# A spectral filter and an MLP side by side: where one row load is issued, and which engine does six additions

## The chip, the cores and the metric

The kernel runs on one core of a Trainium2 chip. The core has five engines with a queue of instructions each: TensorE (PE, matrix products into PSUM, with its weight loads listed apart as PEld), VectorE (DVE), ScalarE (ACT), GpSimd (POOL) and SyncE (SP), which here issues all the DMAs. Each queue is executed in its written order; semaphores hold an instruction until what it reads is there. The metric is the time of one execution on the device in microseconds (us), as the median of several runs.

## The reference

The input x has 2048 rows of 448 numbers. Two branches read its layer norm and are added to it:

```python
x = A_x
xn = _layernorm(x, axis=-1)
return x + _A_ref(xn, A_w_r, A_w_i) + _B_ref(xn, B_w1, B_w2, B_w3, B_w4)
```

Branch A takes a real two-dimensional Fourier transform of xn, multiplies it by a filter and transforms it back. Branch B is an MLP over tokens and channels:

```python
h = _gelu(_layernorm(x, axis=-1) @ w1)
# the four quarters of h's columns are shifted by +1, -1, +2, -2 rows
x1 = x + concatenate([g0, g1, g2, g3], axis=-1) @ w2
return x1 + _gelu(_layernorm(x1, axis=-1) @ w3) @ w4
```

with w1, w2 of 448 x 448, w3 of 448 x 1792 and w4 of 1792 x 448.

## The kernel before

**Blocks and groups.** The 2048 rows are taken as 16 blocks of 128 (row 16a + b belongs to block b), kept in float32 in the tiles `xt`. Most products are made from float16 pairs, a high part (ACT) and the rest (DVE), in two or three passes.

**The opening.** SP issues the loads of x, w1, w2 and w3 in the first 12 us. Blocks are normed in four groups of four (`norm1`), turned, and multiplied by w1 (`w1_unit`, matmuls at L465). The gelu of each block goes as a float16 pair into a small tile `hs` (or a part of `x2mem`), and a transposing DMA (L492) brings it into `h`, from where the products with w2 (L510) take it with its shifts. While transposes are awaited, PE goes on with w1 of the next group.

**The second norm.** `ln2` norms the finished rows of some blocks and writes them as a pair into a staging tile `y`; a transposing DMA (L553) puts them into `x2mem`. Its record `after["b8"]` holds the last instructions of the call for blocks 8 to 11: one on ACT, one on DVE and the DMA transpose of block 11 on SP.

**The channel MLP.** Eight groups G = 0 to 7 of two blocks each take seven steps fp. `front` makes the products with w3 (L435), the gelu (L773) and its float16 pair `hf` (L776 on ACT, L777 on DVE). `back` makes the products with w4 into `acc` (L811). For groups 5 to 7 (`STR`), a scheme with fewer products is used: `forms` combines parts of `hf` into `hgm` (L786 to L788), products go into `cr` and `acc` (L826), and at the last such step `cr` is copied to `cross` (L843), four adds of 128 x 224 combine it (L846) and two adds of 128 x 448 bring it into the result (L850). What the title of the change calls group seven is the seventh of the eight, G = 6.

**The spectral branch.** Steps of it are put between those of the MLP. Each of eight folds takes two blocks: `do_fold` loads their rows of x again (L574), norms them on ACT (L578), and adds and subtracts mirrored columns on POOL (L583 to L586); `step1_in` makes the pair `xh` (L594, L595), and `step1` multiplies it (L604). The folds use four buffers in turn. Three, `xf`, lie in memory that w2 and `h` hold before; the fourth is laid over `hgm`, which is not used until group 5. Then come the products of each chunk of the spectrum, the filter, and the way back (`inv_a`, `inv_b`), at whose end a block's sum is written over its rows (L750), put together with a fresh load of x (L560) and stored.

**What sets the order.** A planner writes each engine's queue: it takes the program's instructions with their dependencies and priorities and simulates them with costs of its own. `prio(FILL)` marks the MLP as work that fills gaps; `prio(EVAC)` puts what empties PSUM first. `behind(key)` adds an order without a semaphore: an instruction in the block is queued after the recorded instruction of the same engine. `PACE` and `FOLD` tie the folds' products and norms so to steps of the MLP. An instruction with no such tie and no dependency can be queued as early as the planner finds its engine free. So it is with the rows of the fourth fold: nothing uses their buffer earlier, and the load stands in SP's queue right after the opening loads, at 11.72 us. Loads of folds one to three follow when their memory comes free, at 99.42 us, between the transposes of blocks 4 to 7 and those of blocks 8 to 11.

Of the kernel before, what the change touches and what calls it, by code (L numbers as in the profile page):

```python
# [16 lines left out]
ALU = mybir.AluOpType  # L17
AX = mybir.AxisListType

S, D, DF, F = 2048, 448, 225, 1792  # L20
# [102 lines left out]
def body(tc, nc, x, wf, w1, w2, w3, w4, c_g, c_n, c_small, out):  # L123
    V, A, P, T, SY = nc.vector, nc.scalar, nc.gpsimd, nc.tensor, nc.sync
    PSUM = bass.MemoryType.PSUM

    @contextlib.contextmanager
    def prio(base):
        kept = tc.cur_priority
        tc.cur_priority = max(base, at.get(base, 0))  # L130
        yield
        at[base] = tc.cur_priority
        tc.cur_priority = kept
# [19 lines left out]
    def bank(tag, name):  # L153
        return ps.tile([128, 512], F32, tag=tag, bufs=2, name=name)
# [10 lines left out]
    def xb(b):  # L165
        g, i = WHERE[b]
        return xt[g][:, i]

    xv = x.rearrange("(a b) d -> a b d", b=NB)
# [54 lines left out]
    cross = x2mem.bitcast(F32)[:, 4 * F:4 * F + 2 * D].rearrange("p (i n) -> p i n", i=2)  # L224
# [171 lines left out]
    after = {}  # L396

    @contextlib.contextmanager
    def behind(*key):
        key = key if len(key) > 1 else key[0]  # L400
        with contextlib.ExitStack() as st:
            for i in after[key]:
                st.enter_context(tc.issue_after(i))
            yield
# [166 lines left out]
    def do_fold(b0):  # L571
        f = xf_buf[b0 // 2 % 4]
        X = f.rearrange("p b s d -> p (b s d)")[:, 0:2 * D + 2].rearrange("p (b d) -> p b d", b=2)
        after["X", b0] = (SY.dma_start(X[:, :, 0:D], xv[:, b0:b0 + 2]).ins,)  # L574
        with behind("f", *FOLD[b0 // 2]):
            for i in range(2):
                x_ = X[:, i, 0:D]
                A.activation(out=x_, in_=x_, func=AF.Identity, scale=xn_scale[b0 + i], bias=xn_bias[b0 + i])  # L578
            A.activation(out=X[:, :, D:D + 1], in_=X[:, :, 0:1], func=AF.Copy)  # L579
        ad = X[:, :, 0:D].rearrange("p b (h d) -> p h b d", h=2)[:, :, :, 0:113]  # L580
        bc = X[:, :, 1:D + 1].rearrange("p b (h d) -> p h b d", h=2)[:, ::-1, :, 223:110:-1]
        u = xr.rearrange("p (a b s d) -> p a b s d", a=2, b=2, s=2)
        P.tensor_tensor(out=u[:, 0], in0=ad, in1=bc, op=ALU.add)  # L583
        P.tensor_tensor(out=u[:, 1], in0=ad, in1=bc, op=ALU.subtract)
        for k, op in ((0, ALU.add), (2, ALU.subtract)):
            i = P.tensor_tensor(out=f[:, :, k:k + 2].rearrange("p b s d -> p s b d"), in0=u[:, :, 0], in1=u[:, :, 1], op=op)  # L586
        after["fold", b0] = (i.ins,)
        for i in range(2):
            folds[b0 + i] = f[:, i].rearrange("p s d -> p (s d)")
# [165 lines left out]
    def crossed(G, fp):  # L755
        return G in STR and (G, fp) not in ((7, 5), (7, 6))
# [3 lines left out]
    def keep(m):  # L760
        after["s", len(slots)] = (m.ins,)
        slots.append(m)
# [28 lines left out]
    def back(G, fp):  # L791
        h = hs.pop((G, fp))
        n = D // 2
        end = 4 if G == 7 else 6
        if fp == 0:
            acc[G] = [bank("acc", f"acc{G}{i}") for i in range(2)]
            if G in STR:
                xs[G] = [bank("tr", f"cr{G}{i}") for i in range(2)]
        if (G, fp) == (7, 5):
            xs[G] = [bank("tr", f"end{i}") for i in range(2)]  # L800
        C = [[(slice(0, D), acc[G][i][:, 0:D], 0, 6)] for i in range(2)]
        if G == 7:
            C[1] = [(slice(0, D), acc[G][1][:, 0:D], 0, 4)]
            if fp > 4:
                C[1] = [(slice(n * k, n * k + n), xs[G][k][:, 0:n], 5, 6) for k in range(2)]
        for i in range(2):
            for r, to, s, e in C[i]:
                with behind("m", G, fp) if (G, fp) == (7, 6) and ("m", G, fp) in after else contextlib.nullcontext():
                    for f in range(2):
                        for hi, wi in ((0, 0),) if crossed(G, fp) else ((0, 0), (0, 1), (1, 0)):  # L810
                            m = T.matmul(to, h[:, hi, 2 * f + i], w4p[0][:, wi, 2 * fp + f, r],  # L811
                                         start=fp == s and f == 0 and hi + wi == 0, stop=fp == e and f == 1 and hi == 1)
                after["m", G, fp] = (m.ins,)
            if not i and not crossed(G, fp):
                yield keep(m)
        if crossed(G, fp):
            g = hg.pop((G, fp))
            X = [xs[G][k // 2][:, n * (k % 2):n * (k % 2) + n] for k in range(4)]
            H = [[acc[G][i][:, n * k:n * k + n] for k in range(2)] for i in range(2)]
            prods = [(0, 1, X[0], 9), (1, 3, H[1][0], 9), (3, 2, H[0][0], C[0][0][3]), (6, 4, X[2], 9),  # L820
                     (4, 5, X[3], end), (5, 6, X[1], end), (2, 7, H[1][1], C[1][0][3])]
            for hi, wi, part in ((0, 1, 0), (1, 0, 0), (0, 1, 1), (1, 0, 1)):
                if hi + part == 1 and wi == part:
                    yield keep(m)
                for k, slot, to, e in prods[3 * part:3 + 4 * part]:
                    m = T.matmul(to, h[:, hi, slot] if slot < 4 else g[:, hi, slot - 4], w4f[fp][k][wi], start=k in (0, 6) and fp == 0 and hi == 0,  # L826
                                 stop=hi == 1 and fp == e)
            after["m", G, fp] = (m.ins,)
        k34 = p34[:, 1:2] if G >= 6 else p34[:, 0:1]
        to = {i: rest[2 * G + i] if G >= 6 else xb(2 * G + i) for i in range(2)} if fp >= 4 else {}  # L830

        def evacuate(i):
            for r, src, _, e in C[i]:
                if fp == e:
                    V.scalar_tensor_tensor(out=to[i][:, r], in0=src, scalar=k34, in1=to[i][:, r], op0=ALU.mult, op1=ALU.add)
                    if G == 7 and fp == 6:
                        SY.dma_start(ov[:, 2 * G + i, r], to[i][:, r])

        with prio(EVAC):
            if G in STR and fp == end:  # L840
                e0, e1 = cross[:, 0], cross[:, 1]
                for i in range(2):
                    A.activation(out=cross[:, i], in_=xs[G][i][:, 0:D], func=AF.Copy, scale=k34)  # L843
                for o, x, y in ((e0[:, n:], e0[:, 0:n], e0[:, n:]), (e1[:, 0:n], e1[:, 0:n], e0[:, n:]),
                                (e0[:, n:], e0[:, n:], e1[:, n:]), (e1[:, n:], e1[:, 0:n], e1[:, n:])):
                    (V if G == 7 else P).tensor_tensor(out=o, in0=x, in1=y, op=ALU.add)  # L846
            for i in range(2):
                evacuate(i)
                if G in STR and fp == end:
                    (V if G == 7 else P).tensor_tensor(out=to[i], in0=to[i], in1=cross[:, 1 - i], op=ALU.add)  # L850
                if G == 6 and fp == 6:
                    SY.dma_start(ov[:, 2 * G + i], to[i])
        yield keep(m)

    def steps(Gs, last=False, hook=None, ahead=1, tags=("mm",)):
        todo = [(G, fp) for G in Gs for fp in range(7)]
        done = formed = 0
        for n, (G, fp) in enumerate(todo):
            while done < min(n + 1 + ahead, len(todo)):
                yield from front(*todo[done], tags[done % len(tags)])  # L860
                if hook:
                    with prio(EVAC):
                        hook(*todo[done])
                done += 1
            while formed < min(n + 2, len(todo)):
                forms(*todo[formed])
                formed += 1
            if fp == 3 and last:
                for b in (2 * G, 2 * G + 1):
                    rest[b] = unscaled(b, x2mem.bitcast(F32)[:, D * (b - 12):D * (b - 11)])  # L870
            yield from back(G, fp)
# [139 lines left out]
    for k in (1, 3):  # L1011
        with behind(0, 3):
            A.activation(out=w2p[:, 0, k], in_=w2s[:112, k], func=AF.Copy)
        with behind("np", 2):
            i = P.tensor_tensor(out=w2p[:, 1, k], in0=w2s[:112, k], in1=w2p[:, 0, k], op=ALU.subtract)
# [95 lines left out]
    for b in range(0, NB, 2):  # L1111
        do_fold(b)
        step1_in(b)
        step1_in(b + 1)
        with behind("m", *PACE[b // 2]):
            step1(b)
            step1(b + 1)
# [80 lines left out]
```

## Time and profile before

| | |
|---|---|
| median of three runs | 410.64 us (409.51 to 411.13) |
| the profiled execution | 409.72 us |
| its span, first to last instruction | 407.6 us |
| PE, DVE, ACT, POOL busy | 401.3, 304.2, 268.6, 179.8 us |
| granted TensorE clock, of full speed | 0.999 |
| moved by DMA | 49.46 MB |

The profile is one execution. The span is shorter than the time by what lies around the instructions. Busy time is the union of an engine's instructions; the matmuls of a stretch overlap in the records, since they are pipelined. A row of the timeline gives start and length in us, engine, line, operation, output and input tile, shape, the number of instructions merged, and in brackets the idle time before it with what ended it. A row of a group gives count, busy us and mean ns. DMA rows on SP show the issue; the landing times are given apart, from issue to the last byte.

### The profile page before, as it was taken

How to read it: one execution, taken by the hardware profiler on the slowest of the kernel's cores; microseconds unless marked ns; L12 is line 12 of the kernel's file. 1: busy time of each engine (PE TensorE's matmuls, PEld its weight loads, DVE VectorE, ACT ScalarE, POOL GpSimd, SP SyncE). 2: the span in 40 equal slices, each digit the busy share in tenths (PEclk: the TensorE clock that was granted, in tenths of full speed). 3: DMA queues.
4: the chain of work that ended last, by engine and by line, in shares of the span. 5: the costliest groups of instructions: out<-in, count | busy, mean ns of one | idle time of the engine just before them, and what ended most of it. 6: DMA issues, size and time to landing. Idle time of an engine off the chain costs nothing.

```text
span 407.6 us, 8828 instructions
## 1 busy us (share of the span) xinstructions
PE 401.3 (98%) x3379; PEld 296.0 (73%) x3379; DVE 304.2 (75%) x658; ACT 268.6 (66%) x465; POOL 179.8 (44%) x276
## 2 busy tenths in 40 slices
PE   8998999999999999999999999999999999999996
PEld 4553555666767777776888887877788888888885
DVE  5988999899653757894577777763488879889645
ACT  4698993884737865763488888785956566544332
POOL 3889723011197747499243344441231254217100
PEclk9999999999999999999999999999999999999999
DMA  8999999915910375317055666642000022323201
GB/s 282 351 274 198 177 180 261 260 23 109 207 48 0 92 233 175 103 36 170 19 135 146 151 145 151 153 112 60 2 2 2 24 68 75 108 70 112 92 2 45
DMA packets 57209, 49.46 MB, mean 121 GB/s; under 512 B 41312, under 2 KB 52192, under 8 KB 57168
## 3 DMA queue, kind: packets, MB, share of 16 engines
q1 hardware_dynamic: 57168, 48.91, 46.4%
q8 instruction: 26, 0.43, 0.5%
q14 instruction: 15, 0.12, 0.1%
HBM read 35.06 MB, written 3.67 MB: 95 GB/s over the span
## 4 chain that ended last, share of the span: by engine, by line
PE 96%; DMA 2%; ACT 1%; DVE 0%; issue 0%; ACTq 0%
PE pw L435 33%; PE acc L811 24%; PE pw L510 9%; PE pw L465 6%; PE cr L826 4%; PE acc L826 3%; PE pu L707 3%; PE ps L604 3%; PE pp L661 2%; PE pe L727 2%; PE px L678 2%; PE py L749 2%; PE wps L889 2%; DMA h<-hs 2%; PE pta L414 1%; PE end L811 1%
## 5 line engine op out<-in xcount | busy, mean ns | idle before, releaser
L435 PE MATMUL pw<-x2mem,w3p 128*128 128x256 f16 x1232 | 149.7, 272 | 0.0
L435 PEld LDWEIGHTS <-w3p 128*128 128x128 f16 x1232 | 118.7, 98 | 19.4
L811 PE MATMUL acc<-w4p,hf 128*128 128x448 f16 x508 | 107.4, 352 | 0.0
L811 PEld LDWEIGHTS <-hf 128*128 128x128 f16 x532 | 51.5, 98 | 35.5
L777 DVE SCALAR_TENSOR_TENSOR hf<-pw,h,hf 128x512 f16<-128x512 f32 x56 | 41.8, 747 | 36.5 <-ACT hf L776 36.3
L773 ACT ACTIVATE pw<-pw,pe 128x512 f32<-128x512 f32 x56 | 36.7, 656 | 44.8 <-PE pw L435 44.6
L510 PE MATMUL pw<-w2p,h 112*128 112x448 f16 x192 | 39.2, 353 | 1.3 <-DMA h<-hs 1.2
L734 POOL TENSOR_TENSOR e<-e 128x226 f32<-128x226 f32 x16 | 11.1, 696 | 63.7 <-ACT e L731 56.2
L776 ACT ACTIVATE hf<-pw,h 128x512 f16<-128x512 f32 x56 | 38.3, 683 | 1.3
L465 PE MATMUL pw<-w1p,w4x 128*128 128x448 f16 x176 | 34.8, 352 | 0.5 <-DVE h L967 0.5
L510 PEld LDWEIGHTS <-h 112*128 112x128 f16 x192 | 18.4, 98 | 18.0 <-DMA h<-hs 2.2
L688 POOL TENSOR_TENSOR xr<-te 128x450 f32<-128x450 f32 x16 | 15.7, 981 | 34.5 <-DVE te L686 34.5
L465 PEld LDWEIGHTS <-w4x 128*128 128x128 f16 x176 | 17.1, 98 | 16.4 <-ACT w4x L424 0.7
L696 POOL TENSOR_TENSOR zb<-xr,zb 128x450 f16<-128x450 f32 x16 | 16.1, 1009 | 16.8 <-ACT zb L695 16.8
L684 DVE SCALAR_TENSOR_TENSOR te<-px,sc,wc 128x450 f32<-128x450 f32 x16 | 11.0, 685 | 10.6 <-ACT te L683 7.0
L683 ACT ACTIVATE te<-px 64x450 f32<-64x450 f32 x32 | 17.2, 538 | 1.7 <-PE px L678 1.2
L719 ACT ACTIVATE U<-y 113x512 f16<-113x512 f16 x32 | 18.0, 620 | 0.1
L741 ACT ACTIVATE vh<-e 128x448 f16<-128x448 f32 x16 | 9.2, 575 | 13.5 <-DVE e L739 13.3
L731 ACT ACTIVATE e<-pe 128x452 f32<-128x452 f32 x16 | 8.7, 545 | 14.0 <-PE pe L727 11.6
L540 POOL TENSOR_SCALAR y<-xt,nm 128x448 f32<-128x448 f32 x6 | 5.9, 986 | 23.3 <-DMA x2mem<-y 12.9
L711 DVE SCALAR_TENSOR_TENSOR y<-pu,y 113x512 f16<-113x512 f32 x16 | 10.9, 687 | 6.9 <-ACT y L710 6.8
L583 POOL TENSOR_TENSOR xr<-xf 128x452 f32<-128x452 f32 x6 | 6.7, 1125 | 20.6 <-ACT xf L579 10.5
(208 smaller groups left out, 799.0 us busy)
## 6 DMA issues: line engine op xcount, KB each, us to landing
wc<-wf SPq DMA_DIRECT2D x32, 225.0 KB, 3.8
wl<-wf SPq DMA_DIRECT2D x8, 450.0 KB, 3.9
xt<-x SPq DMA_DIRECT2D x3, 896.0 KB, 11.3
w3raw<-w SPq DMA_DIRECT2D x3, 896.0 KB, 14.6
xf<-x SPq DMA_DIRECT2D x6, 448.0 KB, 3.7
xr<-x SPq DMA_DIRECT2D x12, 224.0 KB, 2.5
out<-xr SPq DMA_DIRECT2D x12, 224.0 KB, 2.0
gn<-c_g SPq DMA_DIRECT2D x16, 128.0 KB, 3.2
```

Of the source, the lines that this page charges most:

```text
L435: m = T.matmul(ps_out, wp[:, wi + t, cols], xT[:, xi + t, tok], start=t == 0 and wi + xi == 0, stop=t == 3 and wi == 4)
L465: m = T.matmul(pm[:, :D], xTs[g][:, xi + t, 128 * i:128 * i + 128], w1p[:, wi + t], start=t == 0 and p == 0, stop=t == 3 and p == 2)
L510: m = T.matmul(w2b[b][:, :D], hT[g][:112, 4 * hi + k, o:o + 128], w2p[:, wi, k], start=k == 2 and hi + wi == 0, stop=k == 3 and hi == 1)
L683: i = A.activation(out=e[64 * h:64 * h + 64], in_=px_[64 - 64 * h:128 - 64 * h, :2 * DF], func=AF.Copy)
L688: P.tensor_tensor(out=z, in0=t[:, 0], in1=t[:, 1], op=ALU.add)
L696: P.tensor_tensor(out=zv[1], in0=z, in1=zv[0], op=ALU.subtract)
L719: A.activation(out=U[b][:113, p].rearrange("p q (c k) -> p q c k", c=NC), in_=Y1[:113, p, :, :, b], func=AF.Copy)
L773: A.activation(out=pm, in_=pm, func=AF.Gelu_apprx_tanh, scale=r3)
L776: i = A.activation(out=h[:, 0], in_=pv_, func=AF.Copy, scale=h3)
L777: j = V.scalar_tensor_tensor(out=h[:, 1], in0=pv_, scalar=h3, in1=h[:, 0], op0=ALU.mult, op1=ALU.subtract)
L811: m = T.matmul(to, h[:, hi, 2 * f + i], w4p[0][:, wi, 2 * fp + f, r], start=fp == s and f == 0 and hi + wi == 0, stop=fp == e and f == 1 a ...
L826: m = T.matmul(to, h[:, hi, slot] if slot < 4 else g[:, hi, slot - 4], w4f[fp][k][wi], start=k in (0, 6) and fp == 0 and hi == 0, stop=hi ...
```

## The change

Every fold's row load is put behind the recorded instructions of blocks 8 to 11 in the second norm. Since an order of this kind holds between instructions of one engine, the load, which SP issues, is queued after the DMA transpose of block 11. The four half adds and two full adds at the end of group G = 6 go from POOL to DVE, where those of G = 7 are already; G = 5 stays on POOL.

```diff
@@ -571,7 +571,8 @@
     def do_fold(b0):
         f = xf_buf[b0 // 2 % 4]
         X = f.rearrange("p b s d -> p (b s d)")[:, 0:2 * D + 2].rearrange("p (b d) -> p b d", b=2)
-        after["X", b0] = (SY.dma_start(X[:, :, 0:D], xv[:, b0:b0 + 2]).ins,)
+        with behind("b8"):
+            after["X", b0] = (SY.dma_start(X[:, :, 0:D], xv[:, b0:b0 + 2]).ins,)
         with behind("f", *FOLD[b0 // 2]):
             for i in range(2):
                 x_ = X[:, i, 0:D]
@@ -843,11 +844,11 @@
                     A.activation(out=cross[:, i], in_=xs[G][i][:, 0:D], func=AF.Copy, scale=k34)
                 for o, x, y in ((e0[:, n:], e0[:, 0:n], e0[:, n:]), (e1[:, 0:n], e1[:, 0:n], e0[:, n:]),
                                 (e0[:, n:], e0[:, n:], e1[:, n:]), (e1[:, n:], e1[:, 0:n], e1[:, n:])):
-                    (V if G == 7 else P).tensor_tensor(out=o, in0=x, in1=y, op=ALU.add)
+                    (V if G > 5 else P).tensor_tensor(out=o, in0=x, in1=y, op=ALU.add)
             for i in range(2):
                 evacuate(i)
                 if G in STR and fp == end:
-                    (V if G == 7 else P).tensor_tensor(out=to[i], in0=to[i], in1=cross[:, 1 - i], op=ALU.add)
+                    (V if G > 5 else P).tensor_tensor(out=to[i], in0=to[i], in1=cross[:, 1 - i], op=ALU.add)
                 if G == 6 and fp == 6:
                     SY.dma_start(ov[:, 2 * G + i], to[i])
```

## The prediction

> **What bounds the kernel now.** I read the page first (span, busy shares, chain), then the windows view for where TensorE (PE) stands still, then the timelines of PE and the SP queue there, and last the rows of what the diff touches.
>
> ```profile
> span 407.6 us, 8828 instructions
> PE 401.3 (98%) x3379; PEld 296.0 (73%) x3379; DVE 304.2 (75%) x658; ACT 268.6 (66%) x465; POOL 179.8 (44%) x276
> PE 96%; DMA 2%; ACT 1%; DVE 0%; issue 0%; ACTq 0%
> ```
> PE is the bound: 98% busy and 96% of the chain that ended last. The windows below (columns: stretch, its length, busy us and instructions of PE, PEld, DVE, ACT, POOL, granted clock, DMA share, GB/s) say where the rest is.
>
> ```profile
> 30.00:31.00 1.00, 0.90 (x5) 0.28 (x3) 1.00 (x2) 0.39 (x1) 1.00 (x2) 1.00 0.73 168
> 31.00:32.00 1.00, 0.00 (x0) 0.00 (x0) 0.27 (x1) 0.00 (x0) 1.00 (x2) 1.00 1.17 153
> 32.00:33.00 1.00, 0.80 (x4) 0.27 (x5) 0.20 (x1) 0.87 (x2) 1.00 (x5) 1.00 1.28 287
> 34.00:195.00 161.00, 160.99 (x1186) 107.57 (x1185) 124.37 (x264) 112.77 (x187) 88.55 (x137) 1.00 0.60 140
> 195.00:404.00 209.00, 209.00 (x2035) 171.99 (x2034) 153.42 (x310) 133.53 (x236) 66.92 (x78) 1.00 0.29 79
> 404.00:407.60 3.60, 0.37 (x4) 0.12 (x2) 0.76 (x2) 0.00 (x0) 0.00 (x0) 0.84 0.37 127
> ```
> From 34 to 404 us PE is idle for 0.01 us of 370. Between 30 and 33 it is idle for 0.10 + 1.00 + 0.20 = 1.30 us, and at the end there are 3.2 us of last sums and stores, which the diff leaves alone. So the change can win only between 30 and 33 us, and anything it does later can at best cost nothing.
>
> **The change, part by part.** It has three effects: the fourth fold's row load leaves the start of the SP queue; the loads of folds one to three go behind the last transpose of blocks 8 to 11; six additions go from GpSimd (POOL) to VectorE (DVE).
>
> *Part one, the early load.* These rows are the SP queue's timeline, then the landing times of its two last early loads (11.21, 11.72), then PE's timeline.
>
> ```profile
> 11.21 0.47 SPq L219 DMA_DIRECT2D w3raw<-w  x1
> 11.72 0.59 SPq L574 DMA_DIRECT2D hgm<-x  x1
> 26.60 3.89 SPq L492 DMA_TRANSPOSE h<-hs  x1
> 30.59 1.25 SPq L492 DMA_TRANSPOSE h<-hs  x1
> DMA to landing us min/median/max: 18.3/18.3/18.3
> DMA to landing us min/median/max: 18.9/18.9/18.9
> 22.25 8.65 PE L465 MATMUL pw<-w1p,w4x 128*128 128x448 f16 x44
> 32.07 7.56 PE L510 MATMUL pw<-w2p,h 112*128 112x448 f16 x36 [1.17 <-DMA h<-hs]
> ```
> The fourth fold's rows (tile hgm) are the last of the opening loads: they land at 11.72 + 18.9 = 30.62 us, the load before them at 11.21 + 18.3 = 29.51. The second transpose of h then sits on SP for 3.89 us instead of some 1.25, and it gets off at 30.49, just as hgm lands. PE has run out of its other work at 30.90 and waits 1.17 us for these transposes. Without the hgm rows, what the transposes stand behind ends 30.62 - 29.51 = 1.11 us earlier. Bounds on PE's gain: none if the transposes are slow by themselves; at most the 1.30 us of idle time plus what the 36 matmuls at 32.07 lose to late transposes. At the pace of the next row they would take 3 x 2.27 = 6.81 us against 7.56, so 0.75 more, 2.05 in all. I take 1.1, the load's own time, because the release at 30.49 and the landing at 30.62 lie so close.
>
> ```profile
> 72.90 2.27 PE pw L510 x12
> ACT hs L488 <- DMA h<-hs: 1.7, 1, 1.7
> ```
> The gain should last: ScalarE (ACT) waits for the same transposes (1.7 us, second row, from the waits), DVE is nearly idle from 31 to 33, and after 34 PE has no other idle time that could take the gain back. Next late are the following transposes, which move with the first, since they go through the same queue.
>
> The Trainium skill, "DMA: Bandwidth & Descriptors", Queues, rings and completion order, says that each DMA engine consumes the descriptors of a ring in order; the order of landings here agrees (29.51, 30.62, then the transposes). By that rule alone the gain is the 1.1 us of the load; if queued transfers shared the engines, part of the load's time would already be hidden, and the gain would be nearer the lower bound.
>
> *Part two, folds one to four.* SP, then when the first three fold rows landed after issue, the VectorE row that completes block 11, and the first fold's way through ACT and DVE to PE.
>
> ```profile
> 99.42 1.55 SPq L574 DMA_DIRECT2D xf<-x  x3
> 101.09 7.40 SPq L553 DMA_TRANSPOSE x2mem<-y  x4
> DMA to landing us min/median/max: 3.9/4.5/5.4
> 103.91 0.61 DVE L551 SCALAR_TENSOR_TENSOR y<-y,vs 128x384 f16<-128x384 f32 x1
> 108.65 1.40 ACT L578 ACTIVATE xf<-xf,nm,vw 128x448 f32<-128x448 f32 x2
> 115.11 1.79 DVE L595 TENSOR_TENSOR xh<-xf,xh 128x452 f16<-128x452 f32 x2 [0.90 <-ACT xh L594]
> 119.09 1.50 PE L604 MATMUL ps<-csm,xh 128*128 128x128 f16 x24
> 120.43 6.93 PE L435 MATMUL pw<-x2mem,w3p 128*128 128x256 f16 x62
> 123.88 1.40 ACT L578 ACTIVATE xf<-xf,nm,vw 128x448 f32<-128x448 f32 x2
> ```
> The pin holds only SP instructions: all eight loads come behind block 11's transpose, on SP. The four transposes of blocks 8 to 11 now end at 101.09 + 7.40 = 108.49. Without 1.55 us of loads ahead they start earlier, but block 11 is ready only at 103.91 + 0.61 = 104.52, so with 1.25 to 1.9 us each the first load is issued between about 106.4 and 108.5. With 3.9 to 5.4 us to land, the first fold's rows are there between 110.3 and 113.9, in the middle 111.5; ACT took them at 108.65. So this fold is 1.7 to 5.3 us later, 2.9 in the middle. What hides it: its halves are ready at 116.90 and PE starts the second twelve of the 24 matmuls at 119.09 + 0.75, a slack of 2.9 us. Stall: 0 in the middle, 2.4 at the late end; a gain is excluded, since PE is not idle there. The 62 matmuls that come next depend on no fold, and the planner can put some of them first. I take 0 and keep 0 to 2.4. If ACT's queue holds the fold ahead of a gelu, that gelu waits too, and so does PE behind it; that is in the late end. Folds two and three have room: their first use is 123.88 and later, against a landing by some 115. The fourth comes after those and is not needed earlier. Fold five waits for the first fold's buffer, as before, and moves with it; behind it on SP stand only later folds and the filter's loads. On POOL the forms of w4 queued behind the first fold move too; POOL is busy 88.55 of 161 us in that stretch, and the sixth group is the first to use them.
>
> *Part three, group seven's sums* (G = 6 in the code). First the lines of the four half adds and the two full adds on both engines (DVE does this today for the last group), then the two windows in which they run, then DVE's neighbours alone and beside POOL's adds, DVE's last piece without a gap after it, the matmul that follows, and POOL's last add before the sums.
>
> ```profile
> L846 POOL TENSOR_TENSOR x2mem<-x2mem x8: 657/675/1101, 333.1 to 374.8; 128x224 f32<-128x224 f32 x8
> L846 DVE TENSOR_TENSOR x2mem<-x2mem x4: 391/392/393, 398.6 to 399.9; 128x224 f32<-128x224 f32 x4
> L850 DVE TENSOR_TENSOR x2mem<-x2mem x2: 616/617/618, 400.2 to 400.8; 128x448 f32<-128x448 f32 x2
> 372.00:376.00 4.00, 4.00 (x36) 3.29 (x34) 3.95 (x9) 2.07 (x4) 3.61 (x6) 1.00 0.38 115
> 376.00:380.00 4.00, 4.00 (x36) 3.20 (x34) 3.97 (x6) 1.46 (x3) 2.44 (x2) 1.00 0.42 155
> 371.16 0.69 DVE L560 SCALAR_TENSOR_TENSOR xr<-xt,s,xr 128x448 f32<-128x448 f32 x1
> 375.90 1.55 DVE L560 SCALAR_TENSOR_TENSOR xr<-xt,s,xr 128x448 f32<-128x448 f32 x1
> 369.91 0.62 DVE L742 TENSOR_TENSOR vh<-e,vh 128x448 f16<-128x448 f32 x1 [0.64 <-ACT vh L741]
> 374.88 1.09 DVE L742 TENSOR_TENSOR vh<-e,vh 128x448 f16<-128x448 f32 x1
> 381.79 0.29 DVE L788 TENSOR_TENSOR hgm<-hf,hgm 128x256 f16<-128x256 f16 x1
> 382.97 0.45 PE L826 MATMUL cr<-w4x,hgm 128*128 128x224 f16 x3
> 371.31 0.99 POOL L735 TENSOR_TENSOR e<-e 128x226 f32<-128x226 f32 x1
> ```
> DVE gains 4 x 0.392 + 2 x 0.617 = 2.80 us of work, in 8 us where it is already busy for 7.92. It loses the time that its own two-input operations spend beside POOL's adds: 1.55 - 0.69 = 0.86 and 1.09 - 0.62 = 0.47, together 1.33. Net: 1.5 us more. DVE has its first gap at 381.79 + 0.29 = 382.08, and PE reads those forms from 382.97: 0.9 us of slack, so 1.5 - 0.9 = 0.6 if everything behind moves back alike, 2.80 - 0.9 = 1.9 if no stretch goes away. But L560, which only prepares rows for a store, can step behind; PE then loses nothing. A gain is excluded (209.00 of 209.00). I take 0.2, near the lower end because of L560, and keep 0 to 1.9. The freed POOL time is worth nothing: nothing that PE needs follows there.
>
> The stretched rows both read two tiles in SBUF. The Trainium skill, "SBUF — State Buffer", Who interferes with whom, makes that a lock: such an operation and a GpSimd one that reads SBUF block each other for a whole instruction. By that rule the moved sums can themselves stand behind POOL's L735, 0.99 us, which would put part three at 0.6 + 1.0 = 1.6 instead of 0.2. No run here shows a sum of this kind beside it.
>
> **Sum.** -1.1 + 0 + 0.2 = -0.9 us. The profiled execution took 409.72 us (span 407.6, 2.1 around it), so 408.8; the median of the three runs is 0.92 above it, so 410.64 - 0.9 = 409.7.
>
> **The rivals.**
> 1. The load was hidden: the transposes are slow by themselves. For it: the DMA engines move only 153 to 168 GB/s between 30 and 32 us, so not bytes but transposes fill them. Against it: SP's hold ends at hgm's landing. Time: 410.64 + 0.2 = 410.8.
> 2. VectorE becomes the limit at 372 to 383 (the first group of stretched rows does not shrink, L560 is not moved back): 410.64 - 1.1 + 1.9 = 411.4. For it: 7.92 of 8.00 busy. Against: the gaps after 382.
> 3. The other side: the first fold comes too late for PE. Place: the 24 matmuls at 119.09; price 2.4 us; 410.64 - 1.1 + 0.2 + 2.4 = 412.1. It decides once the rows land after 108.65 + 2.9 = 111.6 us and PE's queue keeps its order, and outweighs the early gain from 112.5 on. For it: SP's hold of 7.40 us for four transposes. Against: without the loads in front the rings are emptier.
> 4. The planner lays out another order after 100 us and PE finds heads of its queue not ready. PE is idle for 0.01 us now, so a new order can only lose; three waits like the 1.17 at 32.07 would be 3.5 us: 410.64 - 0.9 + 3.5 = 413.2. For it: every order after the pin is computed from the same plan. Against: most spectral steps stay tied to a slot of the MLP.
>
> **How the numbers follow.** Forecast 0.45, rival one 0.15, two 0.10, three 0.10, four 0.20. About 0.5% (2.05 us) is what a measurement of this kernel can tell from no change: 408.6 to 412.7. Faster than that takes the whole upper bound of part one, or runs that scatter as the three before did (409.51 to 411.13): 0.13, out of the forecast. Slower: most of rival four and the late ends of two and three, 0.22. The rest, 0.65, is within. Range: 408.3 (upper bound of part one, a little scatter) to 413.0; the forecast's own is 408.6 to 410.6.
>
> **What would show it.** Part one: no row load of hgm at 11.7, the second transpose short on SP, PE's first L510 near 31.0, its idle time between 30 and 33 at 0.2 or less. If L510 still begins at 32, part one is wrong. Part two: four fold loads in a row behind the transposes near 106 to 109, ACT's first fold at 110 to 112, no PE idle before the first L604. Part three: L846 and L850 of group seven on DVE at 0.39 and 0.62, L560 near 0.7, POOL empty after about 372, no PE gap from 376 to 384. A PE idle sum above 0.5 us between 34 and 404 would mean that a later cost was missed.

## The result, and the profile after

The changed kernel takes 408.97 us (median of 22 executions, 408.02 to 409.97), the kernel before on the same chips 410.35 us (22 executions, 408.44 to 412.22). The ratio is 0.9969, with an interval of 0.9958 to 0.9981: 0.8 to 1.7 us are gained. The profiled execution took 408.91 us, its span is 406.4 (before 409.72 and 407.6). The forecast started from a median of 410.64, that of the three executions known then, and had a gain of 0.9 us; measured from 410.35 the gain is 1.4 us.

In the changed kernel the lines behind the pin have moved down by one: the row load is L575, the fold's norm L579, its matmuls L605, the half adds L847 and the full adds L851. First the page's span, busy times and chain.

```profile
span 406.4 us, 8829 instructions
PE 401.0 (99%) x3379; PEld 295.9 (73%) x3379; DVE 304.0 (75%) x664; ACT 268.4 (66%) x465; POOL 173.0 (43%) x270
PE 83%; DVE 7%; DMA 3%; ACT 3%; issue 1%; POOL 0%; SPq 0%; DVEq 0%; ACTq 0%
```

PE is still the bound. Its share of the chain falls from 96% to 83% although it is busier than before; the reason is one wait of 0.25 us at 376.98 (below), at which the chain steps from PE over to what PE waited for and follows DVE, ACT and some DMAs back to 333 us. A share of the chain is not a price.

The windows of the changed kernel, with the columns of the prediction's table:

```profile
30.00:31.00 1.00, 1.00 (x7) 0.53 (x6) 1.00 (x2) 1.00 (x3) 1.00 (x2) 1.00 1.02 202
31.00:32.00 1.00, 1.00 (x7) 0.49 (x5) 0.83 (x2) 1.00 (x3) 1.00 (x2) 1.00 0.94 180
32.00:33.00 1.00, 1.00 (x7) 0.50 (x6) 0.89 (x2) 1.00 (x4) 1.00 (x3) 1.00 0.99 181
34.00:195.00 161.00, 161.00 (x1192) 108.07 (x1191) 123.61 (x261) 110.99 (x183) 89.51 (x142) 1.00 0.59 141
195.00:403.00 208.00, 207.75 (x2025) 170.90 (x2023) 152.52 (x314) 133.45 (x236) 59.04 (x70) 1.00 0.29 79
```

The hole between 30 and 33 us is gone: PE is busy for 3.00 of 3.00 us, against 1.70 before. From 34 us on it loses 0.25 us in all, against 0.01. The opening again, from the timelines of SP and PE; the landing time is that of the load issued at 10.72.

```profile
10.72 0.47 SPq L219 DMA_DIRECT2D w3raw<-w  x1
25.00 2.50 SPq L492 DMA_TRANSPOSE h<-hs  x1
28.96 1.28 SPq L492 DMA_TRANSPOSE h<-hs  x1
DMA to landing us min/median/max: 17.5/17.5/17.5
30.70 7.31 PE L510 MATMUL pw<-w2p,h 112*128 112x448 f16 x36
37.85 8.49 PE L465 MATMUL pw<-w1p,w4x 128*128 128x448 f16 x44
```

No row load of hgm stands behind the w3 load any more, and no transpose sits on SP for 3.89 us. The first L510 begins at 30.70 instead of 32.07, and its 36 matmuls take 7.31 instead of 7.56 us. The next run of L465 begins at 37.85; before it began at 39.47. PE is 1.62 us earlier there, and so is SP: its third transpose is issued at 28.96 instead of 30.59.

In 13 of the 14 traces of this case, the second transpose (28.96 is the third) gets off SP within 0.25 us of the landing of the last opening load: before at 30.49 and 30.62, with the pin alone (below) at 28.57 and 28.66. In this trace of the change it is not held: it takes 1.24 us and leaves at 28.85, after the load of w3 has landed at 28.22.

### The profile page after: what moved, and what is told of

It is laid out like the page before. It is cut to its first block, busy times and chain, and to the rows that moved or that the text cites. A ratio compares the mean times of both kernels' runs of the same rounds, so it can differ in the third digit from the quotient of the medians.

```text
span 406.4 us, 8829 instructions
## 1 busy us (share of the span) xinstructions
PE 401.0 (99%) x3379; PEld 295.9 (73%) x3379; DVE 304.0 (75%) x664; ACT 268.4 (66%) x465; POOL 173.0 (43%) x270
## 4 chain that ended last, share of the span: by engine, by line
PE 83%; DVE 7%; DMA 3%; ACT 3%; issue 1%; POOL 0%; SPq 0%; DVEq 0%; ACTq 0%
PE pw L435 28%; PE acc L812 22%; PE pw L510 8%; PE pw L465 6%; PE pu L708 3%; PE ps L605 3%; PE pp L662 2%; PE px L679 2%; PE cr L827 2%; PE acc L827 2%; DVE xr L560 1%; DMA out<-xr 1%; PE pe L728 1%; PE py L750 1%; DVE hf L778 1%
## 5 line engine op out<-in xcount | busy, mean ns | idle before, releaser
L435 PE MATMUL pw<-x2mem,w3p 128*128 128x256 f16 x1232 | 149.2, 272 | 0.0
L435 PEld LDWEIGHTS <-w3p 128*128 128x128 f16 x1232 | 118.8, 98 | 19.4
L510 PE MATMUL pw<-w2p,h 112*128 112x448 f16 x192 | 39.0, 352 | 0.1
L735 POOL TENSOR_TENSOR e<-e 128x226 f32<-128x226 f32 x16 | 11.0, 688 | 64.0 <-ACT e L732 56.5
L465 PE MATMUL pw<-w1p,w4x 128*128 128x448 f16 x176 | 34.8, 352 | 0.5 <-DVE h L968 0.5
L510 PEld LDWEIGHTS <-h 112*128 112x128 f16 x192 | 18.6, 98 | 16.3 <-DMA h<-x2mem 0.9
L465 PEld LDWEIGHTS <-w4x 128*128 128x128 f16 x176 | 17.0, 98 | 16.4 <-ACT w4x L424 0.7
```

The lines of the kernel that those rows point to most:

```text
L435: m = T.matmul(ps_out, wp[:, wi + t, cols], xT[:, xi + t, tok], start=t == 0 and wi + xi == 0, stop=t == 3 and wi == 4)
L465: m = T.matmul(pm[:, :D], xTs[g][:, xi + t, 128 * i:128 * i + 128], w1p[:, wi + t], start=t == 0 and p == 0, stop=t == 3 and p == 2)
L510: m = T.matmul(w2b[b][:, :D], hT[g][:112, 4 * hi + k, o:o + 128], w2p[:, wi, k], start=k == 2 and hi + wi == 0, stop=k == 3 and hi == 1)
```

## The experiments

The times compare with the kernel before on the same chip. This table follows PE's gain through the traces, by the start of three pieces of its work: the run of L465 that follows the first L510, the first fold's first matmul, and the last piece of group G = 7. Line numbers shift by what each kernel adds.

| kernel | L465 | first fold's matmul | last piece of G = 7 |
|---|---|---|---|
| before | 39.47 | 119.09 | 403.06 |
| the change | 37.85 | 117.47 | 401.86 |
| the pin alone | 37.51 | 117.13 | 401.13 |
| the sums alone | 40.11 | 120.17 | 404.14 |
| pin on the fourth fold alone | 37.80 | 117.43 | 401.40 |
| 224 KB early | 38.47 | 118.68 | 403.69 |
| 896 KB early | 41.83 | 121.45 | 405.42 |
| first fold's rows last | 37.90 | 119.71 | 406.38 |
| sums later | 37.79 | 117.41 | 401.38 |

From the first column to the second, PE takes 79.6 us in six of the nine kernels; the sums alone and 224 KB lose 0.4 and 0.6 us there, which no experiment follows, and with the first fold's rows last it is the wait told below.

**Each part alone.** The pin without the sums, run on two chips:

```diff
-                    (V if G > 5 else P).tensor_tensor(out=o, in0=x, in1=y, op=ALU.add)
+                    (V if G == 7 else P).tensor_tensor(out=o, in0=x, in1=y, op=ALU.add)
...
-                    (V if G > 5 else P).tensor_tensor(out=to[i], in0=to[i], in1=cross[:, 1 - i], op=ALU.add)
+                    (V if G == 7 else P).tensor_tensor(out=to[i], in0=to[i], in1=cross[:, 1 - i], op=ALU.add)
```

> The row loads are pinned, group seven's sums stay on GpSimd; only SP's order differs from the kernel before. If the whole gain comes from the early load and the sums on VectorE take part of it back, as the trace after says (PE is 1.6 us ahead until 370 us and 1.2 us at the end): 1.6 us faster than before, ratio about 0.996, first L510 near 30.7 us, and no idle time of PE between 370 and 384. If the sums brought part of the gain: 1.2 us faster or less, ratio 0.997 or more.

> The pin alone once more, sums on GpSimd: 1.6 to 2.0 us faster than before, ratio 0.995 to 0.996.

Measured: 408.66 us, ratio 0.996 (0.9945 to 0.9975), and on the other chip 409.01 us, 0.9968 (0.9951 to 0.9986). That is the whole gain of the change. The second run lies above the 0.995 to 0.996 that was expected of it.

The sums without the pin:

```diff
-        with behind("b8"):
-            after["X", b0] = (SY.dma_start(X[:, :, 0:D], xv[:, b0:b0 + 2]).ins,)
+        after["X", b0] = (SY.dma_start(X[:, :, 0:D], xv[:, b0:b0 + 2]).ins,)
```

> Group seven's sums on VectorE, the row loads as before. If the sums cost: 0.2 to 0.4 us slower than before, ratio 1.0005 to 1.001, first L510 at 32.1 as before, and PE waiting some 0.25 us near 378 for hf of the last group's first step. If the sums help: faster by 0.2 us or more.

Measured: 410.27 us, 1.0004 (0.9987 to 1.0022): nothing. The early load is still there, and so is the wait, in this PE row of its timeline:

```profile
32.80 7.47 PE L510 MATMUL pw<-w2p,h 112*128 112x448 f16 x36 [1.77 <-DMA h<-hs]
```

The pin on the fourth fold only, the sums on POOL:

```diff
-        with behind("b8"):
+        with behind("b8") if b0 == 6 else contextlib.nullcontext():
```

> Only the fourth fold's load is pinned; folds one to three are loaded as before, the sums are on GpSimd. If the later loads of folds one to three cost nothing: the same as the pin alone, 1.6 us faster than before, with the first fold's norm on ACT about 2 us earlier than with all pinned. If their lateness costs: faster than the pin of all, by 0.3 us or more.

Measured: 408.11 us, 0.9947 (0.9929 to 0.9965). All of the gain comes from the fourth fold's early load. By the expectation, a kernel faster than the pin alone by 0.3 us or more would mean that the late loads of the other folds cost something; the median is 0.55 us lower, but the intervals overlap, and in the traces PE takes 79.6 us from L465 to the first fold in both. So no such cost is shown.

The change once more, beside the second run of the pin alone:

> The change itself, beside the next two kernels. If group seven's sums on VectorE cost PE what its profile shows (0.4 us between 375 and 384), it is 0.3 to 0.5 us slower than the pin alone: ratio to before 0.9965 to 0.997. If that wait is one of this execution only: the same as the pin alone, 0.995 to 0.996.

Measured: 408.85 us, 0.9963 (0.9944 to 0.9983), against 0.9968 for the pin alone on that chip. The times can't tell the sums on DVE from the sums on POOL.

**How much is loaded early.** The pin with 224 KB of other rows of x in the place of the 448 KB, and the kernel before with another 448 KB ahead of its early load. The rows go into memory that is free at that time, and nothing uses them.

```diff
+    SY.dma_start(csm.bitcast(F32)[:, 0:D], xv[:, 8])
```

> All loads pinned, sums on GpSimd, and 224 KB of x loaded early at the old place of the fourth fold's rows (the rows are not used). If the cost goes with the bytes: half of the gain is lost, 0.8 us faster than before, first L510 near 31.4. If a transfer of any size at that place costs the whole: as before. If half a load is hidden under PE's other work: 1.3 us faster or more.

```diff
+    SY.dma_start(csm.bitcast(F32)[:, 0:2 * D].rearrange("p (b d) -> p b d", b=2), xv[:, 8:10])
```

> The kernel before with another 448 KB of x loaded early into a tile that is loaded again later (the rows are not used), directly ahead of the fourth fold's. If bytes queued ahead of the transposes cost PE their time: 1.5 us slower than before (1.1 to 2.4), first L510 near 33.6. If the transposes are slow by themselves: as before within 0.4 us, first L510 at 32.

Measured: 409.69 us, 0.9983 (0.9968 to 0.9998), with 224 KB; 412.35 us, 1.0056 (1.0037 to 1.0074), with 896 KB. PE's rows, first with 224 KB, then with 896 KB:

```profile
31.15 7.47 PE L511 MATMUL pw<-w2p,h 112*128 112x448 f16 x36 [0.16 <-DMA h<-hs]
```

```profile
32.89 0.74 PE L511 MATMUL pw<-w2p,h 112*128 112x448 f16 x3 [2.05 <-DMA h<-hs]
```

The kernels without an early load are at L465 at 37.5 to 38.4 us (ten traces, mean 37.9), 224 KB at 38.47, 448 KB at 39.47 and 40.11, 896 KB at 41.83. So 448 KB cost some 1.6 to 2.2 us, and another 448 KB 1.7 to 2.4. But with 896 KB the first L510 begins at 32.89, not near 33.6 as expected, and only 0.1 to 0.8 us later than with 448 KB (32.80 and 32.07). The rest is in the windows of the 896 KB kernel (the granted clock is the third number from the end); the last line is the first of these windows in the kernel with the sums alone, after its wait of 1.77 us:

```profile
34.00:35.00 1.00, 1.00 (x4) 0.42 (x4) 0.52 (x3) 1.00 (x3) 1.00 (x7) 0.56 1.14 226
35.00:36.00 1.00, 1.00 (x5) 0.36 (x3) 1.00 (x4) 1.00 (x3) 1.00 (x4) 0.50 0.98 191
36.00:37.00 1.00, 1.00 (x4) 0.37 (x3) 1.00 (x5) 1.00 (x3) 1.00 (x3) 0.50 0.99 190
37.00:38.00 1.00, 1.00 (x5) 0.49 (x4) 1.00 (x3) 1.00 (x3) 0.82 (x3) 0.74 1.32 132
34.00:35.00 1.00, 1.00 (x7) 0.49 (x5) 0.52 (x3) 1.00 (x4) 1.00 (x8) 1.00 1.12 214
```

With 896 KB early, PE runs at half clock for 3.4 us after its waits, which costs 0.44 + 0.50 + 0.50 + 0.26 = 1.70 us. The windows count PE as busy there, so idle time alone does not show this price. The time of the 224 KB kernel holds something else too: its profiled execution loses 1.04 us at the sums, as shown under part three below.

**The first fold's rows late.** The pin with the sums on POOL, and the four loads in the order two, three, four, one (each behind the one before it). Only SP's order differs from the pin alone.

```diff
+        if b0 == 0:
+            last = "b8"
+            for b1 in (2, 4, 6, 0):
...
+                with behind(*last) if isinstance(last, tuple) else behind(last):
+                    after["X", b1] = (SY.dma_start(X1[:, :, 0:D], xv[:, b1:b1 + 2]).ins,)
+                last = ("X", b1)
```

> As the change with sums on GpSimd, but the first fold's rows are loaded last of the four pinned loads; all other queues keep their order. In the trace after, the first fold's second half is ready 0.6 us before PE reads it. Three loads more in front are 1.5 us of issue and some 3 to 4 us of transfer: the rows land 2 to 4 us later, and PE waits 1.4 to 3.4 us ahead of the first L605, so 0.2 us faster to 1.8 us slower than before. If the rows' lateness is hidden elsewhere: 1.6 us faster, as the pin alone.

Measured: 412.75 us, 1.0038 (1.0003 to 1.0074), where the pin alone has 0.996: about 3.2 us by the two ratios. The rows of its timeline: the load of the first fold's rows, ACT's norm of them, and PE.

```profile
107.40 0.40 SPq L580 DMA_DIRECT2D xf<-x  x1
113.22 1.41 ACT L588 ACTIVATE xf<-xf,nm,vw 128x448 f32<-128x448 f32 x2 [6.04 <-DMA xf<-x]
116.19 0.93 PE L821 MATMUL acc<-w4p,hf 128*128 128x448 f16 x4 [0.90 <-ACT hf L786]
119.71 0.28 PE L614 MATMUL ps<-csm,xh 128*128 128x128 f16 x2 [0.96 <-ACT xh L604]
122.36 8.33 PE L435 MATMUL pw<-x2mem,w3p 128*128 128x256 f16 x62
```

ACT stands for 6.04 us before the fold's rows, with a part of the gelu's pair behind it in its queue; PE waits 0.90 us for that, then 0.96, 0.18 and 0.22 us for the fold itself, 2.26 us in all. Then the clock falls here too:

```profile
122.00:123.00 1.00, 1.00 (x10) 0.81 (x8) 1.00 (x3) 0.40 (x1) 1.00 (x2) 0.50 0.49 41
123.00:124.00 1.00, 1.00 (x6) 0.75 (x5) 0.92 (x2) 0.20 (x1) 1.00 (x2) 0.50 0.81 287
```

With 0.90, 0.50, 0.50, 0.50 and 0.90 from 121 to 126 us the loss is 1.7 us, and the 62 matmuls of L435 take 8.33 instead of 6.93 us. That is the profiled execution, 412.87 us. The four others have a mean clock of 1.000 and still take 411.05 to 412.91 us; what they lose, and where, is not shown by any trace.

**The sums.** Half of them back on POOL: the half adds on DVE, the full adds on POOL.

```diff
-                    (V if G > 5 else P).tensor_tensor(out=to[i], in0=to[i], in1=cross[:, 1 - i], op=ALU.add)
+                    (V if G == 7 else P).tensor_tensor(out=to[i], in0=to[i], in1=cross[:, 1 - i], op=ALU.add)
```

> As the change, but of group seven's sums only the four half adds are on VectorE; the two full adds stay on GpSimd. If what costs is VectorE's work ahead of hf: 1.57 us of work instead of 2.80, PE's wait near 377 smaller than 0.25, 1.4 to 1.6 us faster than before. If the adds on GpSimd stretch VectorE's operations as much as they save: 1.2 us faster.

Measured: 407.84 us, 0.9942 (0.9921 to 0.9962). Then the change with two more full adds on DVE, whose results nothing uses:

```diff
+                    if G == 6:
+                        V.tensor_tensor(out=cross[:, 1 - i], in0=to[i], in1=cross[:, 1 - i], op=ALU.add)
```

> The change with two more full adds on VectorE behind the sums (their results are not used): 1.23 us more in the crowded stretch. If VectorE is the limit there, PE waits longer by as much as is not covered: 0.25 us becomes 0.8 to 1.5, and the kernel is 0.6 to 1.3 us slower than the change. If VectorE has room there: the same as the change.

Measured: 408.51 us, 0.9954 (0.9936 to 0.9972). DVE carries 1.24 us more in that place and the kernel is no slower; PE's wait is the same 0.25 us as in the change:

```profile
377.17 0.27 PE L827 MATMUL cr<-w4p,hf 128*128 128x224 f16 x1 [0.25 <-DVE hf L778]
```

At last all sums on DVE, but two steps later: collected, and put behind the forms of step (7, 2).

```diff
+            if G == 6 and fp == 6:
+                def sums():
+                    half_adds(V)
+                    for i in range(2):
+                        V.tensor_tensor(out=to[i], in0=to[i], in1=cross[:, 1 - i], op=ALU.add)
+                        SY.dma_start(ov[:, 2 * G + i], to[i])
+                later.append(sums)
...
+        if (G, fp) == (7, 2):
+            with behind("f", 7, 2):
+                later.pop()()
```

> All loads pinned, group seven's sums on VectorE, but queued behind hf of the last group's third step (some 384 us), where VectorE has gaps. If the sums cost only because they stand ahead of hf and the forms at 372 to 380: no wait of PE there, 1.6 us faster than before. If 2.8 us more on VectorE cost anywhere: 1.2 us faster, as the change.

> The pin, with the sums on VectorE behind the last group's third step, once more. If the crowded stretch from 370 to 384 costs anything in the other two, this one is the fastest by 0.2 to 0.4 us, ratio 0.9945 to 0.995; if not, all three are the same.

Measured: 408.11 us, 0.995 (0.9931 to 0.9969), and on the other chip 408.06 us, 0.9955 (0.994 to 0.9971). By the medians this, the half adds on POOL and the pin on the fourth fold alone (407.84 to 408.11) are 0.9 to 1.1 us under the 408.97 of the change, but the intervals of their ratios overlap with that of the change; a better version is not shown. On the chip of the second run, 9 of 12 executions with the later sums are under the lowest of the change there (408.46), which speaks for the later sums. In the first of the two runs DVE's operations in that place have their short lengths:

```profile
372.78 0.63 DVE L743 TENSOR_TENSOR vh<-e,vh 128x448 f16<-128x448 f32 x1
373.33 0.68 DVE L560 SCALAR_TENSOR_TENSOR xr<-xt,s,xr 128x448 f32<-128x448 f32 x1
```

## Why the prediction was right, point by point

The time (409.7 forecast, 408.97 measured), the sign and a gain of less than 0.5% came out, and the gain came from where the forecast put it. In the two traces the terms are -1.62, 0 and +0.42, together -1.2 by the spans, against -1.1, 0 and +0.2: two terms were too small and partly cancel, and that much of the closeness is luck. The terms:

**Part one, -1.1 forecast.** The mechanism was right and the size too small. In the two traces PE gains 1.62 us by L465, inside the bound of 2.05; the two traces with 448 KB early and the ten without lie 1.1 to 2.6 us apart there, so 1.1 is the low end. Two things were left out of it. First, the load of w3 ahead of it lands earlier too: at 10.72 + 17.5 = 28.22 now, at 29.51 before. Of these 1.29 us, 0.49 are an earlier issue, and 0.8 a shorter time from issue to landing (17.5 instead of 18.3 us). Without an early load this time is 16.6 to 18.2 us in the ten traces, with 448 or 896 KB behind it 18.3 to 18.5; so the load behind seems to slow the one ahead, though one pair of traces would not show it (in the second run of the pin alone w3 lands at 29.51 as well). The Trainium skill's rule of order in a ring ("DMA: Bandwidth & Descriptors", Queues, rings and completion order) agrees with the order of landings. The case that the prediction set beside it, queued transfers that share the engines, fits the later landing of w3, and it did not bring the gain nearer its lower bound as the prediction had it. Second, the 36 matmuls at L510 no longer wait for later transposes: 7.31 instead of 7.56 us. The view that the step rested on, the landing of hgm beside the end of SP's hold, was right, as the 13 traces show; but the distance between two landings was not the price of the second transfer. Rival one, the hidden load, falls with the pin alone (0.996) and the sums alone (1.0004).

**Part two, 0 forecast.** Right. The rows of the folds in the changed kernel: two lines of loads on SP, the landing of the first two, then ACT, DVE and PE.

```profile
104.94 2.01 SPq L575 DMA_DIRECT2D xf<-x  x3
106.99 0.47 SPq L575 DMA_DIRECT2D hgm<-x  x1
DMA to landing us min/median/max: 4.4/4.4/4.5
109.32 1.41 ACT L579 ACTIVATE xf<-xf,nm,vw 128x448 f32<-128x448 f32 x2 [2.19 <-DMA xf<-x]
115.79 1.79 DVE L596 TENSOR_TENSOR xh<-xf,xh 128x452 f16<-128x452 f32 x2 [2.76 <-ACT xh L595]
117.47 1.50 PE L605 MATMUL ps<-csm,xh 128*128 128x128 f16 x24
```

ACT takes the first fold at 109.32; in the clock of the kernel before, 1.62 us later, that is 110.9, inside the forecast's 110.3 to 113.9. The halves are ready at 117.58 and the second twelve matmuls start at 117.47 + 0.75 = 118.22: of 2.9 us of slack 0.64 are left, and no wait stands before the 24. The 62 matmuls stayed behind them; the planner did not move them ahead as the prediction thought it might. Rival three did not come, but its place is real: with the rows 4 us later PE waited as it said, with the gelu held on ACT. Its price of 2.4 us fits the 2.26 us of waits in that trace, and lacked the 1.7 us of half clock behind them.

**Part three, +0.2 forecast.** Not told apart from zero by the times. Now the rows of the changed kernel at the sums; the last two are of the kernel with the sums alone, which has the same queues of PE, DVE, ACT and POOL (there POOL's line is L735):

```profile
369.66 1.08 DVE L560 SCALAR_TENSOR_TENSOR xr<-xt,s,xr 128x448 f32<-128x448 f32 x1
369.68 0.58 POOL L736 TENSOR_TENSOR e<-e 128x226 f32<-128x226 f32 x1
373.79 0.61 DVE L743 TENSOR_TENSOR vh<-e,vh 128x448 f16<-128x448 f32 x1
374.33 0.67 DVE L560 SCALAR_TENSOR_TENSOR xr<-xt,s,xr 128x448 f32<-128x448 f32 x1
374.92 0.80 DVE L847 TENSOR_TENSOR x2mem<-x2mem 128x224 f32<-128x224 f32 x2
376.18 0.74 DVE L778 SCALAR_TENSOR_TENSOR hf<-pw,h,hf 128x512 f16<-128x512 f32 x1
376.98 0.27 PE L827 MATMUL cr<-w4p,hf 128*128 128x224 f16 x1 [0.25 <-DVE hf L778]
372.25 0.69 DVE L560 SCALAR_TENSOR_TENSOR xr<-xt,s,xr 128x448 f32<-128x448 f32 x1
372.39 0.99 POOL L735 TENSOR_TENSOR e<-e 128x226 f32<-128x226 f32 x1
```

L560 and L743 behind 373 us have shrunk to 0.67 and 0.61 us as forecast, and the sums run at the forecast durations. What this trace loses is 0.25 us of wait, and 0.42 by the table (from L465 to the last piece it lasts 364.01 us instead of 363.59), not in the forms after 382 but at `hf`, which stands behind the half adds on DVE. So the sign "no PE gap from 376 to 384" was not met in this trace. The reason given for the 0.2 did not come: L560 at 374.33 still stands ahead of `hf`. With the sums on DVE two other traces, that of the sums alone and that of the change's second run, lose nothing there. With the sums on POOL the loss is not always nothing either: these are the rows of the second run of the pin alone.

```profile
374.24 2.60 POOL L851 TENSOR_TENSOR x2mem<-x2mem 128x448 f32<-128x448 f32 x2
374.32 1.54 DVE L743 TENSOR_TENSOR vh<-e,vh 128x448 f16<-128x448 f32 x1
375.78 1.55 DVE L560 SCALAR_TENSOR_TENSOR xr<-xt,s,xr 128x448 f32<-128x448 f32 x1
375.91 0.35 PE L750 MATMUL py<-vh,csm 128*128 128x448 f16 x1 [0.30 <-DVE vh L743]
378.05 0.27 PE L827 MATMUL cr<-w4p,hf 128*128 128x224 f16 x1 [0.42 <-DVE hf L778]
```

Here the full adds on POOL hold L743 as well as L560, and PE waits twice and loses 1.05 us in the stretch. "A gain is excluded" was therefore wrong as a sentence: it read PE's 209.00 of 209.00 in one execution as if it held in all. Beside each other's SBUF work DVE and POOL hold each other up as the Trainium skill says ("SBUF — State Buffer", Who interferes with whom), 1.54 against 0.61 us.

What goes with the loss stands just ahead of the sums: an L560 on DVE and POOL's last piece of `e`, which start almost together (369.66 and 369.68 in the change, 372.25 and 372.39 with the sums alone). One of the two is held; in the change it is L560, and the chain back from PE's wait runs over it. Over 13 traces (all but that of the first fold's rows last):

| sums of G = 6 | L560, POOL's piece, us | first fold's matmul to last piece of G = 7, us |
|---|---|---|
| POOL: before, pin alone, pin on the fourth fold, 896 KB | 0.69, 0.99 to 1.03 | 283.97 to 284.00 |
| POOL: pin alone again, 224 KB | 1.09, 0.58 | 285.02, 285.01 |
| DVE: sums alone, the change again | 0.68 to 0.69, 0.99 to 1.04 | 283.97, 283.99 |
| DVE: the change, two more adds | 1.08, 0.58 | 284.39, 284.40 |
| half adds on DVE | 1.09, 0.58 | 284.17 |
| DVE, later: first run | 0.69, 1.03 | 283.97 |
| DVE, later: second run | 1.09, 0.58 | 284.14 |

Where L560 starts 0.09 to 0.15 us ahead of POOL's piece, POOL is held and PE loses nothing; where it is only 0.02 or 0.03 us ahead, DVE is held for 0.4 us, and PE loses 1.05 us with the sums on POOL, 0.42 with the sums on DVE and 0.2 with half of them there or all of them later. So moving the sums costs nothing in one case and saves 0.6 us in the other. What the prediction feared of the lock, a sum behind POOL's last piece, did not come up, since that piece ends at 369.68 + 0.58 = 370.26, before the first sum; the operation that it can hold is L560. Rival two falls with the two further adds: 1.24 us more on DVE cost nothing that the times show.

**Rival four, a new order.** The pin alone changes SP's order only: the lists of PE, DVE, ACT and POOL are the same, instruction for instruction. In the whole change the queues of PE, DVE and POOL differ from those before only between 372 and 383 us, around the six sums; there the planner did lay out PE's products anew, but the sums alone, with the same queues, lose nothing in that place (283.97 in the table).

## What to carry to other kernels

When the bound engine waits at the opening, look at which transfers stand in the queue ahead of the one that it waits for, and whether one of them is not needed until much later: a load without a due time is queued as soon as the planner can, and here 448 KB too early cost 1.6 us of PE. Such a load can be moved to any place with slack; find the slack by the consumer's row (here 2.9 us, of which 2.3 were used). A wait of the bound engine is to be priced with the clock that it may cost afterwards, and an addition moved between DVE and POOL with the time that the two engines hold each other up, not by its duration alone. Where two operations start almost together, one trace shows only one outcome; look at several before a wait is put down to the change.

## What was not expected of the hardware

**The clock falls after waits that are far from long.** With 896 KB early, waits of 2.05 and 0.26 us within 3.1 us were followed by 3.4 us of half clock; with the first fold late, waits of 0.90, 0.96, 0.18 and 0.22 us within 6.3 us did the same in the profiled execution. After one wait of 1.17 us (before) or 1.77 us (the sums alone) the granted clock stayed at 1.00 in the traces. The Trainium skill, "TensorE: Matmul & The Clock Gate", What's actually happening, gives half clock after an idle window of about 3.4 us, and full clock after a busy one of that length. The length of the fall agrees (3.4 us); the entry differs, for no wait here lasts 3.4 us, and the measurement decides. What the entry depends on is not shown.

**The same loss seems to be in the kernel before now and then.** Its executions beside the experiments fall in two kinds: 64 of 79 have a mean granted clock of 0.998 or more and medians of 409.88 to 410.04 us, and 15 have 0.995 or 0.996 and take 411.4 to 413.0. A mean of 0.996 over 410 us is 1.6 us of lost clock, the size of one fall. Of the 99 executions without any early load and with the folds' loads in their order none has it; of the sums alone 1 of 12 has it, with 896 KB early 8 of 10. So by the medians on two chips the early load costs 0.9 to 1.3 us in the usual execution (409.88 and 409.95 against the pin alone at 409.01 and 408.66), and at times, it seems, a fall of the clock on top. Where in those 15 executions the clock fell is not shown, since no trace of them is there.

**What stays open**: what shifts L560 and POOL's piece against each other by the 0.1 us that decides who is held, how often either happens outside the 13 traces, and whether the 0.9 to 1.1 us between the change and the three variants with the lowest medians are real.
